# Splitting the second unit's heads into high and low parts for their scores, in an attention and MLP kernel

## The chip, the cores and the metric

The kernel runs on one core of a Trainium2 chip. The metric is the device time of one execution in microseconds (us). One core has TensorE (matmuls; PE in the profile, its weight loads PEld), VectorE (DVE), ScalarE (ACT), GpSimd (POOL) and SyncE (SP, which issues most of the transfers here). Each engine works through its own list of instructions in order and waits where an instruction needs another engine's or a transfer's result.

## What is computed

Attention with four sink columns and a sliding window of 128, then an MLP with a leaky step, all in float32. The inputs q, k and v have 4 batches, 8 heads, 768 positions and 64 numbers per position; the weights are float64 in memory.

```python
def _attn_ref(q, k, v, n_sink, window):
    scale = 1.0 / np.sqrt(D)
    scores = scale * np.matmul(q, k.transpose(0, 1, 3, 2))
    pos = np.arange(S)
    is_sink = pos[None, :] < int(n_sink)
    rel = pos[:, None] - pos[None, :]
    in_window = (rel >= 0) & (rel < int(window))
    scores = np.where(is_sink | in_window, scores, -1000000000.0)
    scores = scores - np.max(scores, axis=-1, keepdims=True)
    a = np.exp(scores)
    a = a / (np.sum(a, axis=-1, keepdims=True) + 1e-09)
    return np.matmul(a, v).astype(np.float32)
...
x = np.ascontiguousarray(attn_out.transpose(0, 2, 1, 3)).reshape(B * S, H * D)
h = x @ w_in                      # 3072 x 512 by 512 x 2048
g = np.maximum(0.01 * h, h)
return (g @ w_out).astype(np.float32)
```

## The kernel before, in words

**Units.** The work is cut into eight units: a unit is half a batch, 384 positions, that is three tiles of 128 queries, with all eight heads. Unit 0 is the first half of batch 0, unit 1, the "second unit" of this text, its second half. A first-half head needs 392 columns of keys and sinks, a second-half head 524 (`NK`); with 384 columns of queries, one head's tile `qk` has 776 or 908 columns. Queries and keys stand in it twice, in partitions 0 to 63 and 64 to 127.

**Two kinds of attention.** Units 0 and 1 (`EARLY = 2`, lines 419 to 439) work on float32: one float32 matmul per query tile, which the chip runs as two; as every product is summed twice over the 128 partitions, the scale is halved (`scale`, line 254). Their softmax covers 260 columns, two key blocks and the four sinks (`softmax_early`, lines 268 to 278), and their values are float32. From unit 2 on (`attend_late`) a head is split first (`split_head`, lines 224 to 234): ACT casts it to float32r (line 229), POOL subtracts the cast from the original for the lower copy of the keys (line 230) and for the queries (line 232). A score is then two float32r matmuls, of high and of low queries, against keys whose upper copy is high and whose lower copy is low (line 264), and the softmax there is narrower.

**Buffers of a head.** Loads are issued by SyncE (`load_head`, line 202). The tag `qkraw` has one buffer. The tag `qksp` has two, and holds split heads. In units 0 and 1, two of three heads are loaded straight into a `qksp` buffer, where the matmuls read them, and are called `qkn`; the third goes to `qkraw`. `load_next` (lines 217 to 222) sets how far ahead loads are issued: two heads ahead in units 0 and 1, one head ahead later.

**The MLP of a unit** goes in 16 steps (`fc`). In each, twelve matmuls into `h` (line 519), the leaky step `g` on ACT and VectorE (lines 526 and 527), a cast to its high part `gh` on ACT (528), and the low part `gl` by subtraction (529), which POOL does in unit 0's MLP and VectorE later; one step later nine matmuls into `o` (540).

**The weights** are decoded once, beside unit 0's MLP: SyncE loads 512 KB (lines 153 and 154), VectorE builds float32 from the float64 words in three instructions (170, 172, 174), ACT casts to the high part (178), POOL subtracts for the low part (179).

**Order.** Attention of unit 0 and the start of unit 1 run first; then unit u's MLP steps alternate with unit u + 1's attention, by counts of steps. TensorE's list is in the order in which the code issues it. The lists of ACT, VectorE, POOL and SyncE are set by the compiler's scheduler, from a time line of its own. In unit 1 probabilities are transposed on TensorE (lines 336 and 337) into one bank, which ACT's copy `pt` (338) must empty before the next pair. Names: `s` scores, `pe` the probabilities of an early head, `sk` its sink columns, `xh` and `xl` a unit's attention output in two parts, `wi` and `wo` the weights.

Of the kernel before, what the change touches and what calls it, by code (L numbers as in the profile page):

```python
# [21 lines left out]
B, H, S, D = 4, 8, 768, 64  # L22
# [5 lines left out]
T = 3  # L28
NU = 2 * B
EARLY = 2  # L30
TU = T * P
NSK = 4
SKR = P
# [4 lines left out]
NK = (3 * P + 2 * NSK, 4 * P + 3 * NSK)  # L38
NVB = (3, 4)
SCALE = 1.0 / D ** 0.5  # L40
# [71 lines left out]
def fast_path(ctx, tc, cpool, qk, vu, vs, w_in, w_out, out, ident, lim, masks, tri, diag, negm, wmin, wmax):  # L112
# [11 lines left out]

    wz = wpool.tile([P, TU], mybir.dt.bfloat16, name="wz")
    nc.vector.memset(wz, 0.0)
    zeros = iopool.tile([SKR, TU], F32, tag="io", name="zeros")
    nc.vector.memset(zeros, 0.0)
# [66 lines left out]
    def load_head(u, h):  # L195
        b, half = divmod(u, 2)
        early = u < EARLY
        if early and (u * H + h) % 3 < 2:
            raw = apool.tile([P, TU + NK[half]], F32, tag="qksp", name=f"qkn{u}_{h}")
        else:  # L200
            raw = apool.tile([P, TU + NK[half]], F32, tag="qkraw", name=f"qkraw{u}_{h}", bufs=1)
        nc.sync.dma_start(out=raw, in_=qk[half][b, h])
        raws[u, h] = raw
        if h % 2 == 0:
            if early and h % 4:
                vr = apool.tile([P, 4 * P], F32, tag="vsp", name=f"vn{u}_{h}", bufs=1)
            else:
                vr = iopool.tile([P, 4 * P], F32, tag="vraw", name=f"vraw{u}_{h}", bufs=1)
            eng = nc.scalar if early and u + h else nc.sync
            eng.dma_start(out=vr[:, 0:NVB[half] * P], in_=vu[half][b, h // 2])  # L210
            sr = apool.tile([SKR, P], F32, tag="vsraw", name=f"vsraw{u}_{h}", bufs=2)
            eng.dma_start(out=sr, in_=vs[b, h // 2])
            vraws[u, h] = (vr, sr)
# [2 lines left out]

    def load_next(u, h):
        n = u * H + h
        last = n + 2 if n + 2 < EARLY * H else n + 1
        while loaded[0] <= min(last, NU * H - 1):  # L220
            load_head(*divmod(loaded[0], H))
            loaded[0] += 1

    def split_head(u, h):
        half = u % 2
        n = NK[half]
        raw = raws.pop((u, h))
        sp = apool.tile([P, 2 * TU + NK[1]], F32R, tag="qksp", name=f"qksp{u}_{h}")
        nc.scalar.copy(out=sp[:, 0:TU + n], in_=raw[:, 0:TU + n])  # L229
        nc.gpsimd.tensor_tensor(out=sp[D:P, TU:TU + n], in0=raw[D:P, TU:TU + n],  # L230
                                in1=sp[D:P, TU:TU + n].bitcast(F32), op=ALU.subtract)
        nc.gpsimd.tensor_tensor(out=sp[:, TU + n:2 * TU + n], in0=raw[:, 0:TU],  # L232
                                in1=sp[:, 0:TU].bitcast(F32), op=ALU.subtract)
        return sp
# [13 lines left out]
    raws = {}  # L248
# [2 lines left out]
    warm = ps_h.tile([P, 512], F32, tag="h", name="warm")  # L251

    def scale(u):
        return -SCALE / 2 if u < EARLY else -SCALE

    def scores(u, h, j, parts, sp):
        k0, kn = KSL[u % 2][j]
        i = (h * T + j) % (SO + 1)
        if u == 0 and i:
            ps = ps_o.tile([P, 512], F32, tag=f"o{i - 1}", name=f"s{u}_{h}_{j}")  # L260
        else:
            ps = ps_s.tile([P, 512], F32, tag="s", name=f"s{u}_{h}_{j}")
        for c, off in enumerate(parts):
            nc.tensor.matmul(ps[:, 0:kn], lhsT=sp[:, off + j * P:off + (j + 1) * P],  # L264
                             rhs=sp[:, TU + k0:TU + k0 + kn], start=c == 0, stop=c == len(parts) - 1)
        return ps

    def softmax_early(u, h, j, ps, w, sm):
        half = u % 2
        if half or j:  # L270
            src, mask = ps[:, 0:W3], wide[0 if u == 0 and j == 1 else 1]
        else:
            src, w, mask = ps[:, 0:P], w[:, WM:], masks[0]
        col = (u * H + h) * T + j
        neg = negm[:, col:col + 1]
        anchor[0] = nc.vector.tensor_tensor_reduce(out=w, in0=src, in1=mask, scale=scale(u), scalar=3.0e38,  # L276
                                                   op0=ALU.add, op1=ALU.min, accum_out=neg)
        nc.scalar.activation(out=w, in_=w, func=AF.Exp, scale=-1.0, bias=neg, accum_out=sm[:, j:j + 1])

    def normalise_early(u, w, sm):  # L280
        nc.vector.tensor_scalar(out=sm, in0=sm, scalar1=1e-9, scalar2=None, op0=ALU.add)
        nc.vector.reciprocal(out=sm, in_=sm)
        for j in range(T):
            p = w[:, j, :] if u % 2 or j else w[:, j, WM:]
            if u:
                nc.scalar.mul(p, p, sm[:, j:j + 1])
            else:
                nc.vector.tensor_scalar(out=p, in0=p, scalar1=sm[:, j:j + 1], scalar2=None, op0=ALU.mult)

    def softmax(u, h, j, ps, w):  # L290
        if KSL[u % 2][j][1] == W3:
            nc.vector.copy_predicated(out=ps[:, WM:W3], mask=tri, data=ps[:, 0:P])
            src = ps[:, P:W3]
        else:
            src = ps[:, 0:P]
            w = w[:, NSK:]
        col = (u * H + h) * T + j
        sm = apool.tile([P, 1], F32, tag="sm", name=f"sm{u}_{h}_{j}", bufs=4)
        neg = negm[:, col:col + 1]
        anchor[0] = nc.vector.tensor_tensor_reduce(out=w, in0=src, in1=masks[min(T * (u % 2) + j, 2)],  # L300
                                                   scale=scale(u), scalar=3.0e38, op0=ALU.add, op1=ALU.min,
                                                   accum_out=neg)
        nc.scalar.activation(out=w, in_=w, func=AF.Exp, scale=-1.0, bias=neg, accum_out=sm)  # L303
        nc.vector.tensor_scalar(out=sm, in0=sm, scalar1=1e-9, scalar2=None, op0=ALU.add)
        nc.vector.reciprocal(out=sm, in_=sm)
        if NACT >> u & 1:
            nc.scalar.mul(w, w, sm)
        else:
            nc.vector.tensor_scalar(out=w, in0=w, scalar1=sm, scalar2=None, op0=ALU.mult)  # L309
# [21 lines left out]
    def tail_early(u, h, j, w, pt, sk):  # L331
        half = u % 2
        tp = slot()
        at = (P if half else 0) + (2 * j - 1) * P
        if half or j:
            nc.tensor.transpose(out=tp[:, 0:P], in_=w[:, j, 0:P], identity=ident)  # L336
            nc.tensor.transpose(out=tp[:, P:2 * P], in_=w[:, j, WM:], identity=ident)  # L337
            nc.scalar.copy(out=pt[:, 0, at:at + 2 * P], in_=tp[:, 0:2 * P])
        else:
            nc.tensor.transpose(out=tp[:, 0:P], in_=w[:, j, WM:], identity=ident)  # L340
            nc.scalar.copy(out=pt[:, 0, 0:P], in_=tp[:, 0:P])
        if j == T - 1:
            nj = T - 1 + half
            nc.gpsimd.tensor_copy(out=sk[:, 0:nj, h % 2], in_=w[:, T - nj:, P:WM])
# [20 lines left out]
    def sinks(u, pair, sk):  # L365
# [10 lines left out]
        sv = sv.rearrange("p j q -> p (j q)")  # L376
        if u < EARLY:
            return sv
# [6 lines left out]
    def values(u, h, pt, st, state):  # L385
# [5 lines left out]
        vv, sv = state["v"]  # L391
        if u < EARLY:
            if not odd:
# [11 lines left out]
        for c, (l, r, o, m) in enumerate(mms):  # L405
            nc.tensor.matmul(out[:, o:o + m], lhsT=l, rhs=r, start=c == 0, stop=c == len(mms) - 1,  # L406
                             skip_group_check=True)
        if u < EARLY:
            x = state["acc"][:, 0:TU]
# [8 lines left out]

    def attend_early(u, h, pend, state):
        odd = h % 2  # L420
        sp = raws.pop((u, h))
        state = state[h // 2 % 2]
        if not odd:
            state["v"] = vraws.pop((u, h))
            state["sk"] = apool.tile([P, T, 2, NSK], F32, tag="sk", name=f"sk{u}_{h // 2}")
        load_next(u, h)
        w = apool.tile([P, T, W3], F32, tag="pk", name=f"pe{u}_{h}", bufs=PKB)
        sm = apool.tile([P, T], F32, tag="sm", name=f"sm{u}_{h}", bufs=4)
        pt = apool.tile([P, 1, 2 * TU], F32, tag="pt", name=f"pt{u}_{h}")
        sk = state["sk"]  # L430
        state["pt", odd] = pt
        for j in range(T):
            softmax_early(u, h, j, scores(u, h, j, (0,), sp), w[:, j, :], sm)
            if j < T - 1:
                yield j
        normalise_early(u, w, sm)
        yield T - 1
        for j in range(T):
            pend.append((0, lambda j=j: tail_early(u, h, j, w, pt, sk)))
# [340 lines left out]
```

## Time and profile before

| | |
|---|---|
| median of 3 runs | 749.14 us (748.79 to 749.92) |
| the profiled execution's own time | 746.63 us |
| its span in the profile | 745.1 us |
| mean granted TensorE clock | 0.992 |
| loads of heads into `qkraw` | 26 of 388 KB (first halves), 27 of 454 KB (second halves) |
| split heads | 48 of 64 |

A row of the profile's groups gives the line of the kernel, the engine, the operation, the tile written and the tiles read with their shapes, how often it ran, then its busy time in us and the mean in ns, then the idle time of the engine just before these instructions and what ended it. The chain of waits goes back from the last instruction: at each step to what released it. A row of a time line has start and duration in us, engine, line, operation and count, and in brackets the idle time before it and what ended that. Matmuls overlap, so the duration of a single one is longer than the time for which it holds up the next; the chain gives the latter.

### The profile page before, as it was taken

What the parts mean: (1) busy time and instruction counts of PE and PEld (TensorE: products, weight loads), DVE (VectorE), ACT (ScalarE), POOL (GpSimd) and SP (SyncE); (2) the same over time, 40 slices, a digit from 0 to 9 for tenths busy, and PEclk for the clock granted to TensorE, in tenths of its full rate; (3) what the DMA queues carried; (4) which work ended last, traced back from release to release, by engine and by line L of the source; (5) the groups of instructions that cost most, each with busy time, mean ns of one, the idle gap of its engine ahead of it and who ended that gap; (6) DMA issues with size and microseconds to landing.
All of it is one profiled execution on the core that took longest, in us unless ns stands there. A gap on an engine that the chain in (4) does not pass through costs nothing.

```text
span 745.1 us, 12489 instructions
## 1 busy us (share of the span) xinstructions
PE 714.3 (96%) x3881; PEld 620.6 (83%) x3881; DVE 549.3 (74%) x1749; ACT 420.6 (56%) x1178; POOL 370.0 (50%) x500
## 2 busy tenths in 40 slices
PE   4788999899999999999999999999999999999996
PEld 3446777679999988999988888999889899989995
DVE  6856798847667888888888888889888978733222
ACT  3556567656665666666666666666666655522221
POOL 2303446745445677665666587665666555300000
PEclk9899999999999999999999999999999999999999
DMA  8744675413212343225333443334332321001001
GB/s 295 228 132 127 195 219 172 146 36 99 58 51 65 119 125 114 92 94 156 115 106 102 132 130 100 104 98 153 109 109 78 112 68 40 0 1 43 1 1 48
DMA packets 43755, 77.77 MB, mean 104 GB/s; under 512 B 3616, under 2 KB 26400, under 8 KB 43680
## 3 DMA queue, kind: packets, MB, share of 16 engines
q1 hardware_dynamic: 41520, 74.66, 32.1%
q10 hardware_dynamic: 2160, 2.23, 1.2%
q8 instruction: 33, 0.54, 0.3%
q14 instruction: 42, 0.34, 0.2%
HBM read 70.58 MB, written 6.29 MB: 103 GB/s over the span
## 4 chain that ended last, share of the span: by engine, by line
PE 84%; DVE 9%; ACT 3%; issue 1%; DMA 1%; ACTq 0%; SPq 0%; DVEq 0%
PE o L540 32%; PE h L519 31%; PE v L406 10%; PE s L264 7%; PE t L349 2%; DVE gl L529 2%; DVE zeroi L192 1%; PE t L336 1%; DMA qkn<-in_qk 1%; DVE g L527 1%; DVE pe L276 0%; DVE xf L415 0%; DVE pk L309 0%; PE t L370 0%; PE t L337 0%
## 5 line engine op out<-in xcount | busy, mean ns | idle before, releaser
L519 PE MATMUL h<-xh,wi 128*128 128x384 f32 x1024 | 314.9, 354 | 1.6 <-DVE g L527 1.6
L540 PE MATMUL o<-wo,gh 128*128 128x512 f32 x768 | 244.4, 399 | 0.0
L519 PEld LDWEIGHTS h<-xh,wi 128*128 128x128 f32 x1024 | 190.0, 188 | 16.6 <-issue 2.9
L519 PE MATMUL h<-xl,wi 128*128 128x384 f32 x512 | 172.5, 337 | 0.0
L540 PE MATMUL o<-wo,gl 128*128 128x512 f32 x384 | 151.5, 394 | 0.0
L540 PEld LDWEIGHTS o<-wo,gh 128*128 128x128 f32 x768 | 133.7, 188 | 18.2 <-issue 2.4
L318 POOL TENSOR_SCALAR_AFFINE_SELECT pt<-stg 128x256 fp32r<-128x256 f32 x240 | 101.3, 447 | 83.4 <-DVE stg L357 70.1
L527 DVE TENSOR_TENSOR g<-h,g 128x384 f32<-128x384 f32 x128 | 71.0, 555 | 62.2 <-ACT g L526 60.4
L529 DVE TENSOR_TENSOR gl<-g,gh 128x384 fp32r<-128x384 f32 x112 | 93.3, 833 | 16.5 <-ACT gh L528 15.0
L526 ACT ACTIVATE g<-h 128x384 f32<-128x384 f32 x128 | 62.2, 486 | 71.5 <-PE h L519 71.1
L519 PEld LDWEIGHTS h<-xl,wi 128*128 128x128 f32 x512 | 96.9, 189 | 3.6 <-DVE xl L475 0.2
L230 POOL TENSOR_TENSOR qksp<-qkraw,qksp 64x392 fp32r<-64x392 f32 (+1 forms) x48 | 58.4, 1218 | 64.2 <-issue 47.5
L540 PEld LDWEIGHTS o<-wo,gl 128*128 128x128 f32 x384 | 72.2, 188 | 16.7 <-DVE gl L529 0.3
L303 ACT ACTIVATE pk<-pk,negm 128x128 f32<-128x128 f32 (+1 forms) x144 | 58.1, 403 | 48.6 <-DVE negm L300 47.8
L528 ACT CAST gh<-g 128x384 fp32r<-128x384 f32 x128 | 65.7, 513 | 33.7 <-DVE g L527 31.3
L264 PEld LDWEIGHTS s<-qksp 128*128 128x128 f32 x288 | 53.3, 188 | 5.9
L264 PE MATMUL s<-qksp 128*128 128x260 f32 (+1 forms) x288 | 56.2, 277 | 0.0
L232 POOL TENSOR_TENSOR qksp<-qkraw,qksp 128x384 fp32r<-128x384 f32 x48 | 53.5, 1115 | 3.6
L356 ACT CAST stg<-t 128x128 fp32r<-128x128 f32 x120 | 30.8, 256 | 42.6 <-PE t L349 32.2
L406 PEld LDWEIGHTS v<-pt,vsp 128*128 128x128 f32 x336 | 45.1, 189 | 5.8 <-issue 3.3
L229 ACT CAST qksp<-qkraw 128x776 fp32r<-128x776 f32 (+1 forms) x48 | 42.8, 892 | 11.3 <-PE s L264 11.0
L309 DVE TENSOR_SCALAR pk<-pk,sm 128x132 f32<-128x132 f32 (+1 forms) x120 | 46.0, 383 | 2.4
(131 smaller groups left out, 1088.0 us busy)
## 6 DMA issues: line engine op xcount, KB each, us to landing
qkraw<-in_qk SPq DMA_DIRECT2D x27, 454.0 KB, 3.3
qkraw<-in_qk SPq DMA_DIRECT2D x26, 388.0 KB, 3.1
wiraw<-in_w_in SPq DMA_DIRECT2D x16, 512.0 KB, 3.9
woraw<-in_w_out SPq DMA_DIRECT2D x16, 512.0 KB, 4.0
ciraw<-in_w_in SPq DMA_DIRECT2D x16, 512.0 KB, 3.8
coraw<-in_w_out SPq DMA_DIRECT2D x16, 512.0 KB, 3.6
out<-ob SPq DMA_DIRECT2D x23, 256.0 KB, 2.0
vraw<-in_vu SPq DMA_DIRECT2D x12, 256.0 KB, 2.7
```

The source lines that it names most:

```text
L230: nc.gpsimd.tensor_tensor(out=sp[D:P, TU:TU + n], in0=raw[D:P, TU:TU + n], in1=sp[D:P, TU:TU + n].bitcast(F32), op=ALU.subtract)
L232: nc.gpsimd.tensor_tensor(out=sp[:, TU + n:2 * TU + n], in0=raw[:, 0:TU], in1=sp[:, 0:TU].bitcast(F32), op=ALU.subtract)
L264: nc.tensor.matmul(ps[:, 0:kn], lhsT=sp[:, off + j * P:off + (j + 1) * P], rhs=sp[:, TU + k0:TU + k0 + kn], start=c == 0, stop=c == len(pa ...
L303: nc.scalar.activation(out=w, in_=w, func=AF.Exp, scale=-1.0, bias=neg, accum_out=sm)
L318: nc.gpsimd.affine_select(out=out, in_=src, pattern=([[0, x]] if x > 1 else []) + [[sign, P]], base=-1 if prev else 0, channel_multiplier= ...
L406: nc.tensor.matmul(out[:, o:o + m], lhsT=l, rhs=r, start=c == 0, stop=c == len(mms) - 1, skip_group_check=True)
L519: nc.tensor.matmul(ph[:, 0:TU], lhsT=w[:, cs], rhs=x, start=cc == 0 and c == 0, stop=cc == NCC - 1 and c == 2)
L526: nc.scalar.mul(g, ph[:, 0:TU], 0.01)
L527: anchor[0] = nc.vector.tensor_tensor(out=g, in0=ph[:, 0:TU], in1=g, op=ALU.max)
L528: nc.scalar.copy(out=gh, in_=g)
L529: (nc.gpsimd if u == 0 else nc.vector).tensor_tensor(out=gl, in0=g, in1=gh.bitcast(F32), op=ALU.subtract)
L540: nc.tensor.matmul(po[t], lhsT=gg[:, tsl], rhs=w, start=f == 0 and c == 0, stop=f == NFC - 1 and c == 2)
```

## The change

A new constant `NATS = 1` says how many units read their heads in float32. Unit 0 stays as it was. Unit 1 is now treated in two ways: its softmax over 260 columns, its normalisation, its transposes and its float32 values stay; its heads are loaded into `qkraw`, split by `split_head`, and scored by two float32r matmuls per tile, with the whole scale.

```diff
+NATS = 1
...
     def load_head(u, h):
...
-        if early and (u * H + h) % 3 < 2:
+        if u < NATS and h % 3 < 2:
             raw = apool.tile([P, TU + NK[half]], F32, tag="qksp", name=f"qkn{u}_{h}")
         else:
             raw = apool.tile([P, TU + NK[half]], F32, tag="qkraw", name=f"qkraw{u}_{h}", bufs=1)
...
     def load_next(u, h):
         n = u * H + h
-        last = n + 2 if n + 2 < EARLY * H else n + 1
+        last = n + 2 if n + 2 <= NATS * H else n + 1
...
     def scale(u):
-        return -SCALE / 2 if u < EARLY else -SCALE
+        return -SCALE / 2 if u < NATS else -SCALE
...
     def attend_early(u, h, pend, state):
-        sp = raws.pop((u, h))
+        sp = raws.pop((u, h)) if u < NATS else split_head(u, h)
+        parts = (0,) if u < NATS else (0, TU + NK[u % 2])
...
-            softmax_early(u, h, j, scores(u, h, j, (0,), sp), w[:, j, :], sm)
+            softmax_early(u, h, j, scores(u, h, j, parts, sp), w[:, j, :], sm)
```

`split_head` is called for unit 1 as it stands for the later units:

```python
        sp = apool.tile([P, 2 * TU + NK[1]], F32R, tag="qksp", name=f"qksp{u}_{h}")
        nc.scalar.copy(out=sp[:, 0:TU + n], in_=raw[:, 0:TU + n])
        nc.gpsimd.tensor_tensor(out=sp[D:P, TU:TU + n], in0=raw[D:P, TU:TU + n],
                                in1=sp[D:P, TU:TU + n].bitcast(F32), op=ALU.subtract)
        nc.gpsimd.tensor_tensor(out=sp[:, TU + n:2 * TU + n], in0=raw[:, 0:TU],
                                in1=sp[:, 0:TU].bitcast(F32), op=ALU.subtract)
```

TensorE's list keeps its order; the 24 float32 scores of unit 1 become 24 pairs. In the lists of the other engines the new instructions are put in, and neighbours change places. Line numbers of the kernel after are one or two higher. Three places follow. The first is ACT's list where unit 0's MLP begins, before; `g_0`, `gh_0` are the first step's, `pe_1` is unit 1's head 1, `pt_0` a copy for head 0.

```order
L526 ACTIVATE g_0_663<-h_0_646 128x384
L278 ACTIVATE pe_1_622,sm_1_623<-pe_1_622,negm 128x260
L528 CAST gh_0_664<-g_0_663 128x384
L286 ACTIVATE pe_1_622<-pe_1_622,sm_1_623 128x260 x3
L178 CAST wi_686<-wif_682 128x512
L338 COPY pt_0_586<-t_706 128x256
```

The same place after:

```order
L528 ACTIVATE g_0_674<-h_0_657 128x384
L230 CAST qksp_3_878<-qkraw_3_754 128x908
L279 ACTIVATE pe_1_631,sm_1_632<-pe_1_631,negm 128x260
L530 CAST gh_0_675<-g_0_674 128x384
L179 CAST wi_698<-wif_694 128x512
L287 ACTIVATE pe_1_631<-pe_1_631,sm_1_632 128x260 x3
L339 COPY pt_0_584<-t_718 128x256
```

The cast of unit 1's head 3 stands between the first `g` and what followed it, and the weight cast has gone ahead of the normalisation. The second place is POOL's list from the last heads of unit 0 to the MLP's first low part `gl_0`, before:

```order
L344 COPY sk_2_397<-pe_5_442 128x2x4
L344 COPY sk_3_487<-pe_6_494 128x2x4
L344 COPY sk_3_487<-pe_7_532 128x2x4
L344 COPY sk_0_577<-pe_0_584 128x3x4
L529 TENSOR_TENSOR gl_0_665<-g_0_663,gh_0_664 128x384
```

And after:

```order
L345 COPY sk_2_397<-pe_5_442 128x2x4
L231 TENSOR_TENSOR qksp_0_575<-qkraw_0_488,qksp_0_575 64x524
L233 TENSOR_TENSOR qksp_0_575<-qkraw_0_488,qksp_0_575 128x384
L345 COPY sk_3_487<-pe_6_494 128x2x4
L345 COPY sk_3_487<-pe_7_530 128x2x4
L231 TENSOR_TENSOR qksp_1_621<-qkraw_1_580,qksp_1_621 64x524
L233 TENSOR_TENSOR qksp_1_621<-qkraw_1_580,qksp_1_621 128x384
L345 COPY sk_0_579<-pe_0_582 128x3x4
L231 TENSOR_TENSOR qksp_2_749<-qkraw_2_625,qksp_2_749 64x524
L233 TENSOR_TENSOR qksp_2_749<-qkraw_2_625,qksp_2_749 128x384
L231 TENSOR_TENSOR qksp_3_878<-qkraw_3_754,qksp_3_878 64x524
```

The subtracts of four heads stand ahead of `gl_0` (the fourth head's second one follows the last row). The third place is SyncE's list of loads, unit 1's heads 0 to 4 and the next weights, before:

```order
L202 DMA qkraw_0_488<-in_qk 128x908
L202 DMA qkn_1_530<-in_qk 128x908
L202 DMA qkn_2_578<-in_qk 128x908
L202 DMA qkraw_3_620<-in_qk 128x908
L202 DMA qkn_4_738<-in_qk 128x908
L153 DMA wiraw_829<-in_w_in 128x4x256
L154 DMA woraw_839<-in_w_out 128x1024
```

And after:

```order
L203 DMA qkraw_0_488<-in_qk 128x908
L203 DMA qkraw_1_580<-in_qk 128x908
L203 DMA qkraw_2_625<-in_qk 128x908
L203 DMA qkraw_3_754<-in_qk 128x908
L154 DMA wiraw_844<-in_w_in 128x4x256
L203 DMA qkraw_4_882<-in_qk 128x908
L155 DMA woraw_854<-in_w_out 128x1024
```

All loads of unit 1 share the one `qkraw` buffer, and head 4's load has moved behind one weight transfer.

## The prediction

> **What bounds the kernel now.** I read the head of the page first, then its chain of waits, then a table of busy times in stretches of 20 us around the second unit, last the instructions one by one. Of the page, the span, the busy times and the chain:
>
> ```profile
> span 745.1 us, 12489 instructions
> PE 714.3 (96%) x3881; PEld 620.6 (83%) x3881; DVE 549.3 (74%) x1749; ACT 420.6 (56%) x1178; POOL 370.0 (50%) x500
> ...
> PE 84%; DVE 9%; ACT 3%; issue 1%; DMA 1%; ACTq 0%; SPq 0%; DVEq 0%
> ```
>
> TensorE sets the end, so what counts is what the change does to TensorE's time or makes it wait for. The second unit's scores run from 50 to 138 us. In these stretches stand the busy times of PE, PEld, DVE, ACT and POOL (instructions in brackets), then the granted clock, the transfers' share and GB/s:
>
> ```profile
> 40.00:60.00 20.00, 17.23 (x83) 10.18 (x82) 10.11 (x45) 11.96 (x44) 0.76 (x4) 1.00 0.44 127
> 60.00:80.00 20.00, 18.07 (x95) 14.79 (x93) 16.88 (x37) 13.04 (x34) 9.71 (x10) 1.00 0.59 178
> 80.00:100.00 20.00, 19.54 (x98) 15.70 (x98) 14.82 (x34) 12.00 (x32) 9.98 (x10) 1.00 0.66 184
> 100.00:120.00 20.00, 20.00 (x101) 15.58 (x99) 15.86 (x36) 12.19 (x33) 10.45 (x11) 1.00 0.65 197
> 120.00:140.00 20.00, 19.30 (x96) 14.71 (x94) 15.93 (x33) 12.86 (x32) 13.11 (x13) 1.00 0.68 211
> ...
> 180.00:200.00 20.00, 20.00 (x114) 18.11 (x114) 13.22 (x47) 13.22 (x39) 10.22 (x15) 1.00 0.16 44
> ```
>
> From 80 us on TensorE is nearly full at full clock: a shorter score shows in the end time. From 40 to 80 us it has 4.7 us of gaps: there the order of the other engines decides.
>
> **What the change takes away.** A score of 260 columns is two matmuls before and after. The chain gives what the pair holds up TensorE, first in float32 (second unit), then split (third unit):
>
> ```profile
> 69.91 0.44 PE s L264 x2
> ...
> 162.26 0.24 PE s L264 x2
> ```
>
> That is 0.20 us for each of 8 heads x 3 tiles: 24 x 0.20 = 4.8 us less, the whole gain.
>
> **What it adds.** The third unit and those after it split their heads already, so the prices are there: cast, lower half of the keys, queries, then the load of one head (454 KB, issue to landing; the second row is from 36 to 160 us alone).
>
> ```profile
> L229 ACT CAST qksp<-qkraw 128x908 fp32r<-128x908 f32 x24 | 22.7, 948 | 4.7 <-PE s L264 4.7
> L230 POOL TENSOR_TENSOR qksp<-qkraw,qksp 64x524 fp32r<-64x524 f32 x24 | 32.9, 1371 | 33.3 <-issue 25.3 <-POOL pt L318 7.9
> L232 POOL TENSOR_TENSOR qksp<-qkraw,qksp 128x384 fp32r<-128x384 f32 x48 | 53.5, 1115 | 3.6
> qkraw<-in_qk SPq DMA_DIRECT2D x27, 454.0 KB, 3.3
> qkraw<-in_qk SPq DMA_DIRECT2D x3, 454.0 KB, 3.7
> ```
>
> By volume this fits: ACT gets 8 x 0.95 = 7.6 us, POOL 8 x (1.37 + 1.12) = 19.9 us, over some 80 us in which (60 to 140) POOL has 43 busy and ACT 50. What does not fit by itself is the sequence. All loads of the unit now go into one buffer, which is free only after the second subtract of the head before. A head thus costs at least 3.3 + 0.95 + 1.37 + 1.12 = 6.7 us (7.1 at 3.7 us a load) in a row. Where TensorE takes longer than that per head it is hidden. At the unit's start it does not, and there ACT's order has a cast ahead of work that TensorE needs. The rows for this, SyncE's loads, ACT, TensorE and POOL of before:
>
> ```profile
> 40.00 0.33 SPq L202 DMA_DIRECT2D qkraw<-in_qk  x1
> 43.47 5.86 SPq L202 DMA_DIRECT2D qkn<-in_qk  x2
> ...
> 43.30 0.51 ACT L278 ACTIVATE pe<-pe,negm 128x260 f32<-128x260 f32 x1
> 43.72 0.19 ACT L278 ACTIVATION_READ_ACCUMULATOR pe<-pe,negm 128x1 f32 x1
> ...
> 51.38 0.51 ACT L278 ACTIVATE pe<-pe,negm 128x260 f32<-128x260 f32 x1 [0.52 <-DVE negm L276]
> 51.80 0.19 ACT L278 ACTIVATION_READ_ACCUMULATOR pe<-pe,negm 128x1 f32 x1
> ...
> 61.49 0.49 ACT L526 ACTIVATE g<-h 128x384 f32<-128x384 f32 x1 [0.82 <-PE h L519]
> ...
> 63.47 0.51 ACT L528 CAST gh<-g 128x384 fp32r<-128x384 f32 x1 [0.46 <-DVE g L527]
> ```
>
> ```profile
> 50.16 0.60 PE L264 MATMUL s<-qkraw 128*128 128x260 f32 x2
> ...
> 53.87 0.70 PE L264 MATMUL s<-qkn 128*128 128x260 f32 x2 [0.20 <-DVE negm L276]
> ...
> 58.74 0.44 PE L519 MATMUL h<-xh,wi 128*128 128x384 f32 x1
> ...
> 66.43 0.33 PE L336 MATMUL t<-ident,pe 128*128 128x128 f32 x1 [0.34 <-ACT pt L338]
> ...
> 67.17 0.39 PE L540 MATMUL o<-wo,gl 128*128 128x512 f32 x1
> ...
> 68.09 0.60 PE L264 MATMUL s<-qkn 128*128 128x260 f32 x2
> ...
> 67.04 0.33 SPq L154 DMA_DIRECT2D woraw<-in_w_out  x1
> ...
> 64.06 1.01 POOL L529 TENSOR_TENSOR gl<-g,gh 128x384 fp32r<-128x384 f32 x1 [6.81 <-ACT gh L528]
> ```
>
> Head by head, counted in the second unit:
>
> Head 0: its load stands where it stood (40.00, landed 43.3). The cast comes behind the exponential that ends at 43.9, is done at 44.9, the subtracts at 47.4. TensorE wants it at 50.16: hidden, with 2.8 us to spare; a load that lands later than that costs TensorE the rest in full.
>
> Head 1: its load went out with the pair of 43.47, now only at 47.4; it lands at 50.7. The cast stands behind the exponential that ends at 52.0: done at 52.9, the subtracts at 55.4. TensorE wants it at 53.87, and its second matmul waits for the last subtract: about 1.0 us late, 0.8 when the next, shorter score is through. The MLP thus begins near 59.5 where it began at 58.74.
>
> Head 2: load at 55.4, landed 58.7 to 59.1, cast until 59.7 or 60.1, subtracts until 62.2 or 62.6. Its first score stands at 68.09: hidden by over 5 us.
>
> Head 3: load at 62.2 to 62.6, landed 65.5 to 66.3. Its scores are far off, but ACT takes its cast right behind the first leaky step (61.49), ahead of an exponential, the cast gh, a weight cast, a normalisation and the copy that frees the transposes' bank. ACT stands still from about 63 until the load is there, casts for 0.95, does the exponential in 0.70, and comes to gh at 67.2 to 67.9 where it was there at 63.47: 3.7 to 4.5 us late, I take 4.1. The copy and the transpose at 66.43 come as much later, and TensorE's list has nothing else ahead of them. The MLP's low part gl, now behind head 3's subtracts on POOL, is done near 66.9 + 2.5 + 1.0 = 70.4; TensorE wants it at 67.17 + 4.1 = 71.3: hidden, by 0.9. On SyncE the load of head 4 still stands ahead of the weight transfer of 67.04, but now waits for head 3's subtracts, 69.4: 2.4 us later for the weights while the stage is 4.1 late, so hidden too.
>
> So at this transpose TensorE is 4.1 us late, with the first six cheaper scores in that. The other 18 give back 18 x 0.20 = 3.6. That leaves +0.5.
>
> After it, heads 4 to 7 put four casts ahead of ACT's copies. Bounds: TensorE's waits for these copies fall away by half of what they are below, -1.0; or all four casts reach TensorE, 4 x 0.95 = +3.8. From 180 to 200 us casts of this kind run under a TensorE that is busy 20.00 of 20, so I stay near nothing: +0.5. The transfers add no bytes. The last wait of the stage, for the weights' decode, stays:
>
> ```profile
> PE t L336 <- DVE wof L174: 2.0, 1, 2.0
> PE t L336 <- ACT pt L338: 1.9, 4, 0.7
> ```
>
> Sum: +0.5 + 0.5 = +1.0 us. The profiled execution took 746.63 us (its span of 745.1 and 1.5 around it), which makes 747.6; the median of the runs, 749.14, lies 2.5 above it, so the forecast is 750.1 us. A change of 0.2%, 1.5 us, is about what a measurement of this kernel can tell from none.
>
> A rule speaks against this change. Of the two subtracts' kind POOL needs 1115 ns for 128x384, VectorE 577:
>
> ```profile
> L475 DVE TENSOR_TENSOR xl<-xf,xh 128x384 fp32r<-128x384 f32 x20 | 11.5, 577 | 0.0
> ```
>
> The Trainium skill ("GPSIMD Engine Reference", section 4.1 Engine selection) gives elementwise work to VectorE, since GpSimd is about two times slower with two inputs; the trace agrees, 1115 against 577. By it, subtracts on VectorE would shorten the two links before head 3's cast by some 1.2 us each, and the sum would be about -1.4 (an estimate).
>
> **The rivals.**
>
> Faster: ACT's halt costs TensorE nothing, because loads land sooner than 3.3 us or the waits of 60 to 80 us (1.9) take it up. Then only head 1's 0.8 is lost (five scores in it) and 19 x 0.20 = 3.8 won: -3.0, 746.1 us. For it: TensorE waits there already. Against it: the cast is ahead of gh in a list that keeps its order.
>
> Slower: POOL becomes late in every head. The gl of 64.06 is done at 65.07 and wanted at 67.17: 2.1 us of room, and a head's subtracts take 2.49. If heads 4 to 7 each lose these 0.4 and their cast's 0.95, that is 5.4 us, and with +0.5 before it 755.0 us. It decides when gl ends after the last matmul ahead of its own. Against it: POOL has half its time free.
>
> VectorE held up by POOL. One small step of VectorE, three numbers per row, takes 0.16 us, but 0.78 and 0.86 where a POOL subtract runs beside it:
>
> ```profile
> 63.35 0.16 DVE L281 TENSOR_SCALAR sm<-sm 128x3 f32<-128x3 f32 x1
> 75.73 0.78 DVE L281 TENSOR_SCALAR sm<-sm 128x3 f32<-128x3 f32 x1
> 140.29 0.86 DVE L281 TENSOR_SCALAR sm<-sm 128x3 f32<-128x3 f32 x1 [0.25 <-ACT pe L278]
> ...
> 75.19 1.29 POOL L179 TENSOR_TENSOR wo<-wof,wo 128x512 fp32r<-128x512 f32 x1
> ```
>
> With 19.9 us more of POOL all eight could take 0.7 more, 5.6 us of VectorE; a third of it in the decode that TensorE waits for would add 2 us: 752.1 us. The Trainium skill ("SBUF — State Buffer", section SBUF: two separate sides) calls the port pair that the two share an exclusive lock, held for a whole instruction; the trace agrees, the step of 75.73 ends at 76.51, with POOL's subtract at 76.48.
>
> **How the numbers follow.** Forecast 0.56; its own range -1 to +3, so 0.35 of it within 1.5 us and 0.21 above. Faster rival 0.25. POOL late 0.12, slower. VectorE held up 0.07, 0.05 slower and 0.02 within. Together faster 0.25, same 0.37, slower 0.38. The range takes in the faster rival's -3.0 with a little of its spread and most of the way to the slower one's +5.9: 745.6 to 754.0.
>
> **What would show it.** In the profile of after: scores of the second unit at 0.24 in the chain; ACT waiting some 2 to 3 us for a DMA ahead of the cast near 63 to 66 us; TensorE waiting some 3 us for ACT's copy near 67 to 70 us, and 1 us for POOL near 54; after 80 us no more gaps than before. The forecast is wrong if ACT's cast finds its load landed, if TensorE has waits for gl or weights between 80 and 140 us, or if the wait of 2.0 near 148 us grows.

## The result, and the profile after

The changed kernel takes 753.19 us, median of 4 runs (751.2 to 754.42), the kernel before 748.97 beside it: a ratio of 1.0053, 95% interval 1.0037 to 1.0069. It is slower by about half a per cent. The forecast was 750.1, within a range of 745.6 to 754.0; so the time lies inside the range, but near its upper edge, and what the profile shows is not what the forecast had described.

The head of the page and the shares of the chain, after:

```profile
span 749.3 us, 12515 instructions
PE 717.0 (96%) x3881; PEld 621.7 (83%) x3881; DVE 551.4 (74%) x1749; ACT 425.9 (57%) x1186; POOL 388.4 (52%) x516
...
PE 84%; DVE 8%; ACT 4%; issue 1%; POOL 1%; DMA 1%; ACTq 0%; SPq 0%; POOLq 0%; DVEq 0%
```

ACT has 5.3 us more than before and POOL 18.4, near the 7.6 and 19.9 that were forecast. But TensorE, which lost 4.8 us of scores, is busy 2.7 us longer. Where that is from shows in the stretches of 20 us, with the columns as in the prediction (PE, PEld, DVE, ACT, POOL, then the granted clock):

```profile
40.00:60.00 20.00, 16.69 (x70) 9.47 (x69) 11.25 (x43) 13.77 (x44) 5.90 (x9) 0.85 0.32 99
60.00:80.00 20.00, 17.21 (x75) 13.85 (x75) 10.82 (x24) 9.97 (x26) 9.27 (x10) 0.81 0.34 119
80.00:100.00 20.00, 19.32 (x100) 14.83 (x100) 15.93 (x36) 12.89 (x32) 13.45 (x13) 1.00 0.65 196
100.00:120.00 20.00, 19.95 (x105) 15.53 (x104) 16.69 (x36) 13.36 (x34) 14.50 (x15) 1.00 0.71 221
120.00:140.00 20.00, 18.83 (x100) 14.89 (x99) 17.66 (x38) 14.12 (x37) 16.50 (x16) 1.00 0.71 224
```

The granted clock is 0.85 and 0.81 in the first two rows; before it was 1.00 in both. In finer stretches (TensorE's busy time, then the clock), after:

```profile
52.00:54.00 2.00, 1.51 (x8) 1.00 0.00 0
54.00:56.00 2.00, 1.18 (x3) 0.53 0.00 0
56.00:66.00 10.00, 10.00 (x27) 0.50 0.38 126
66.00:68.00 2.00, 2.00 (x9) 0.55 0.00 0
```

From 54.1 to 67.8 us TensorE runs at half clock: 27 matmul records fill ten microseconds that held 42 before. The fall comes just ahead of head 1's first score, 0.4 us into TensorE's wait for its subtract. TensorE's rows there, after:

```profile
51.35 0.51 PE L265 MATMUL s<-qksp 128*128 128x260 f32 x2 [0.64 <-DVE negm L277]
...
54.33 0.58 PE L265 MATMUL s<-qksp 128*128 128x260 f32 x1 [0.58 <-POOL qksp L231]
55.40 0.58 PE L265 MATMUL s<-qksp 128*128 128x260 f32 x1 [0.49 <-POOL qksp L233]
55.92 2.40 PE L407 MATMUL v<-pt,vn 128*64 128x256 f32 x6
...
63.38 0.69 PE L521 MATMUL h<-xh,wi 128*128 128x384 f32 x1
```

The wait for POOL's two subtracts is there, 0.58 + 0.49 us, as forecast (1.0). Behind it the same six matmuls of the values take 2.40 us that took 1.30 before:

```profile
54.51 1.30 PE L406 MATMUL v<-pt,vn 128*64 128x256 f32 x6
```

and the MLP's first matmul stands at 63.38 where it stood at 58.74: 4.6 us late, where 0.8 was forecast. ACT's list in the place where it was to stand still, after:

```profile
68.00 0.49 ACT L528 ACTIVATE g<-h 128x384 f32<-128x384 f32 x1 [1.50 <-PE h L521]
68.39 0.94 ACT L230 CAST qksp<-qkraw 128x908 fp32r<-128x908 f32 x1
```

The cast of head 3 comes right behind the first leaky step, as forecast, but at 68.39, and it waits for nothing: the load, issued at 61.9, has landed in the time that the slow TensorE took. TensorE's waits from 40 to 165 us, after:

```profile
PE t L337 <- ACT pt L339: 3.3, 4, 1.2
PE t L337 <- DVE wof L175: 1.8, 1, 1.8
```

For ACT's copies it waits 1.4 us more than before, and 1.2 at the longest, not 3 or more. The wait for the weights' decode is nearly the same (1.8, before 2.0). The scores are as short as forecast, and casts and subtracts of the later heads stand on the chain between 80 and 105 us. From the chain of waits of 68 to 140 us:

```profile
79.99 0.26 PE s L265 x2
80.27 0.47 ACT qksp L230
81.35 1.33 POOL qksp L231
82.77 1.01 POOL qksp L233
...
89.15 0.24 PE s L265 x2
95.24 0.85 ACT qksp L230
...
104.75 0.54 ACT qksp L230
```

To compare kernels stage by stage, I take the start of the MLP's 1st, 25th and 145th `h` matmul from TensorE's rows. Between the last two lie the last 17 of the 24 scores, all but the first of heads 2 to 7. By the forecast's terms they save 17 x 0.20 = 3.4 us and the later heads lose 0.5 of it.

| us | 1st | 25th | 145th | 25th to 145th | span |
|---|---|---|---|---|---|
| before | 58.7 | 69.2 | 138.9 | 69.7 | 745.1 |
| after | 63.4 | 76.2 | 143.8 | 67.7 | 749.3 |

The loss is complete by the 25th matmul (7.0 us); 2.0 us come back, not 2.9; from the 145th on the two nearly keep their distance, 4.9 there and 4.2 at the end. Head 0's second score still stands at the same time in both, 51.40 before and 51.35 after; where other runs come to it earlier or later, I count from there.

### The profile page after: what moved, and what is told of

Its sections match the earlier page's. It is cut to its first block, busy times and chain, and to the rows that moved or that the text cites. A ratio compares the mean times of both kernels' runs of the same rounds, so it can differ in the third digit from the quotient of the medians.

```text
span 749.3 us, 12515 instructions
## 1 busy us (share of the span) xinstructions
PE 717.0 (96%) x3881; PEld 621.7 (83%) x3881; DVE 551.4 (74%) x1749; ACT 425.9 (57%) x1186; POOL 388.4 (52%) x516
## 4 chain that ended last, share of the span: by engine, by line
PE 84%; DVE 8%; ACT 4%; issue 1%; POOL 1%; DMA 1%; ACTq 0%; SPq 0%; POOLq 0%; DVEq 0%
PE h L521 32%; PE o L542 32%; PE v L407 11%; PE s L265 6%; PE t L350 2%; DVE gl L531 2%; DVE zeroi L193 1%; PE t L337 1%; ACT qksp L230 1%; DMA qkn<-in_qk 1%; ACT pe L279 1%; DVE g L529 1%; DVE xf L416 0%; DVE pk L310 0%; PE t L371 0%
## 5 line engine op out<-in xcount | busy, mean ns | idle before, releaser
L231 POOL TENSOR_TENSOR qksp<-qkraw,qksp 64x524 fp32r<-64x524 f32 (+1 forms) x56 | 69.0, 1232 | 78.6 <-issue 49.3
L265 PEld LDWEIGHTS s<-qksp 128*128 128x128 f32 x336 | 62.3, 190 | 10.1 <-DVE negm L277 1.2
L265 PE MATMUL s<-qksp 128*128 128x260 f32 (+1 forms) x336 | 67.3, 281 | 1.8 <-DVE negm L277 0.6
L233 POOL TENSOR_TENSOR qksp<-qkraw,qksp 128x384 fp32r<-128x384 f32 x56 | 61.6, 1100 | 4.2
L230 ACT CAST qksp<-qkraw 128x908 fp32r<-128x908 f32 (+1 forms) x56 | 50.4, 900 | 14.8 <-PE s L265 13.8
```

## The experiments

**The theories.** The clock: a pause near 54 us, of about a microsecond, lets TensorE's granted clock fall to half for some 12 us, which costs about 5 us; without it, ACT's stop for head 3's load would appear, as forecast, and cost about as much. The rival: the casts and subtracts cost it, as work that ACT and POOL do in the same stretch. Twelve kernels ran in three groups of four, each group with the kernel before beside it (medians 749.42, 748.3 and 749.25); each ratio is to the kernel before of the same group.

The first theory is tested with spare matmuls: bf16, 128x384, on zeros, into a PSUM bank whose contents nobody reads. They add TensorE work and take nothing away.

```
def fill(n):
    if n:
        pw = ps_o.tile([P, 512], F32, tag="o0", name=f"fill{len(fills)}")
        ...
        for _ in range(n):
            nc.tensor.matmul(pw[:, 0:TU], lhsT=wz[:, 0:P], rhs=wz, start=True, stop=True)
```

**Fourteen spare matmuls** in the changed kernel, ahead of scores of heads 0 and 1:

```
+FILL = (0, 4, 4), (6, 0, 0)
...
+            if u == 1 and h < 2:
+                fill(FILL[h][j])
             softmax_early(u, h, j, scores(u, h, j, parts, sp), w[:, j, :], sm)
```

> The changed kernel with 14 spare matmuls (bf16, 128x384, of zeros, into a bank of o that is free there) in TensorE's list: 4 each ahead of the second and third score of the second unit's head 0, 6 ahead of head 1's first score. They remove no wait and no work; the scheduler also moves a few rows of ACT, POOL and SyncE there. Theory (clock): in the changed kernel TensorE's granted clock falls to 0.50 from about 54 to 67 us because TensorE pauses around 51 to 55 us; with the pauses filled it stays at 1.00, the MLP begins near 60 to 61 us instead of 63.4, and the time is 747 to 749 us against 753.2 of the changed kernel. Rival (ACT and POOL): the loss is the splits' work on ACT and POOL, and the clock is a bystander: the time stays at 753 us or rises by up to 1 us with the spare matmuls.

749.66 us, 1.0004 of before (0.9991 to 1.0017): the whole loss is gone, by adding work. The clock is 1.00 from 54 to 76 us. But this kernel differs in a second way: the scheduler moved rows of ACT's list, the cast of head 3 to a later place among them, and head 3's subtracts on POOL behind the MLP's first low part. So the next one holds the lists.

**Two spare matmuls**, `FILL = (0, 1, 0), (1, 0, 0)`, with the lists of ACT, POOL, VectorE and SyncE exactly those of after:

> The same with two spare matmuls alone, one ahead of the second score of head 0, one ahead of head 1's first; the lists of all other engines are those of the changed kernel. 0.32 us of spare work fills little of the 2 us of pauses. Theory (clock): near the limit, so either the drop stays (753 us) or it is gone (748 us), together with the clock in the table of windows: time and clock go together. Rival (ACT and POOL): 753 us whatever the clock does.

754.91 us, 1.0079 (1.0063 to 1.0094): slower than after. The clock held, 1.00 from 54 to 70 us, and the MLP began at 61.2. Then came what the forecast had described. ACT's cast of head 3 and TensorE's longest wait in this kernel:

```profile
68.08 0.95 ACT L231 CAST qksp<-qkraw 128x908 fp32r<-128x908 f32 x1 [3.65 <-DMA qkraw<-in_qk]
```

```profile
PE t L338 <- ACT pt L340: 7.1, 4, 4.9
```

ACT stands still for 3.65 us for the load, and TensorE 4.9 at the transpose behind its copy (forecast: 2 to 3, and 4.1). After this pause the clock fell all the same, later. TensorE's busy time and clock:

```profile
70.00:72.00 2.00, 0.00 (x0) 1.00 0.01 4
72.00:74.00 2.00, 0.75 (x3) 0.59 0.85 242
74.00:76.00 2.00, 2.00 (x6) 0.50 1.03 357
```

So the two losses stand in each other's way: in after, the low clock delays TensorE until the load has landed; hold the clock up, and the stop is there.

**The same fourteen in the kernel before**, the control:

> Control: the kernel before with the same 14 spare matmuls at the same places. Its clock is 1.00 from 40 to 76 us already, so there is nothing to keep up. Theory (clock): no gain, 749 to 751 us (14 x 0.16 = 2.2 us of matmuls, 1 us of it inside waits). Rival (ACT and POOL): the same. If it is clearly faster than 749, spare matmuls do something else than hold the clock there, and the first run does not count for the theory.

750.37 us, 1.0028 (1.0009 to 1.0047). In the profile (749.36 us) the clock stays up, and the spare matmuls win nothing. Four of the twelve runs, with a mean clock of 0.986 and 0.987, take 753.15 to 754.89; where these lose is not shown.

**Heads 0 and 1 in float32**, as before the change, heads 2 to 7 split:

```
-NATS = 1
+NATH = 10
...
-        if u < NATS and h % 3 < 2:
+        if u * H + h < NATH and (u * H + h) % 3 < 2:
...
```

> The changed kernel with heads 0 and 1 of the second unit left in float32, loaded ahead as in the kernel before; heads 2 to 7 are split. This takes away TensorE's wait for POOL near 54 us and makes TensorE busier there. Theory (clock): the clock stays at 1.00; 18 of the 24 shorter scores are left, 18 x 0.20 = 3.6 us, less up to 1.5 us for casts and subtracts of six heads in TensorE's way: 745.5 to 747.5 us. Rival (ACT and POOL): six of eight splits cost six eighths of the loss: 749.0 + 3.2 = 752 us.

749.26 us, 0.9999 (0.9982 to 1.0017). TensorE waits no more for POOL at 54 us, the clock is 1.00 from 40 to 76, and 25th to 145th takes 67.5 us, near after's 67.7. With six of eight heads split, the loss is gone: it came with the first two, though their casts, subtracts, shorter scores and order of loads went together here. No more is won, and neither expectation held: the theory had 745.5 to 747.5, the rival 752.

**Only heads 0 and 1 split**, the rest as before, was to be the other half of that test:

> The kernel before with only heads 0 and 1 of the second unit split (cast, two subtracts, shorter scores); heads 2 to 7 stay float32 and load ahead as before, so nothing of ACT's stop for head 3's load can occur. Theory (the clock): TensorE waits about 1 us for POOL at 54 us, the granted clock falls to 0.50 from about 54 to 67 us, the 24 v and s matmuls there take twice as long, the MLP starts near 63.4 instead of 58.7 us, and no more than 6 x 0.20 = 1.2 us comes back: 753 to 755 us, 4 to 5 us above the kernel before, although only a quarter of the change is in it. Rival (the work on ACT and POOL costs by its volume, a quarter of it here): 749.5 to 751 us, the clock at 1.00 from 54 to 67.

758.09 us, 1.0113 (1.0089 to 1.0138), slower than either theory said. The edit brought a wait of its own. SyncE's list now has head 2's load ahead of head 1's, and that one waits for its buffer until 50.59; both go out together, and ACT's cast of head 1 waits for the load until 56.04. TensorE's longest wait there is 3.8 us:

```profile
PE s L268 <- DVE sm L285: 3.8, 1, 3.8
```

The row names VectorE, but VectorE's step L285 had itself waited for ACT. The clock then is 0.50 to 0.55 from 58 to 72 us. With **two spare matmuls** in this kernel

> The kernel of e5_two_split with two spare bf16 matmuls of 128x384 on TensorE ahead of heads 0's second and 1's first score; the lists of all other engines are the same. Theory (the clock): the spare matmuls keep the granted clock at 1.00 from 54 to 70 us as in e1b_two_fills, the wait for POOL of about 1 us stays, no stop of ACT follows since head 3's load is early: 749 to 750.5 us, 4 us under e5_two_split. Rival (work on ACT and POOL): spare matmuls add 0.3 us and win nothing: as e5_two_split or above it.

it takes 757.49 us (1.0111, 1.0089 to 1.0133): two matmuls of 0.16 us do nothing against a pause of 4.5. As a test of a short pause both kernels failed. What they show is that a quarter of the change can cost 9.8 us, over twice what all of it costs, so its price does not go by the volume of casts and subtracts alone; the order of the loads, which this edit changed, can cost more.

**The clock held and head 3's cast put later.** The kernel with two spare matmuls, and the cast behind the copy that frees the transposes' bank, five places down ACT's list (a wait on the same engine only):

```
-        nc.scalar.copy(out=sp[:, 0:TU + n], in_=raw[:, 0:TU + n])
+        behind = copied.get((1, 0, 1)) if (u, h) == (1, 3) else None
+        with tc.issue_after(behind.ins) if behind else nullcontext():
+            nc.scalar.copy(out=sp[:, 0:TU + n], in_=raw[:, 0:TU + n])
```

> The kernel of e1b_two_fills (all eight heads split, two spare matmuls that keep the clock up at 54 us) with head 3's cast put five places later in ACT's list, behind the copy that frees the transposes' bank; SyncE's load of head 4 moves behind one weight load. Theory (ACT's stop at head 3's load is what e1b_two_fills lost, and the clock fell after it): the wait of 4.9 us for ACT's copy goes to under 1.5 us, the granted clock stays at 1.00 from 54 to 80 us, the MLP's 25th matmul starts near 71.5 instead of 78.0 us: 748 to 750 us, 5 to 6 us under e1b_two_fills. Rival (the sum of casts and subtracts costs it, wherever they stand): 753 to 755 us.

747.93 us, 0.9995 of before (0.9978 to 1.0011), where the kernel with the two spare matmuls alone had 1.0079: some 6 us less, with every cast and subtract still in it. The scheduler moved more than the cast: head 3's subtracts on POOL go behind the MLP's first low part, and SyncE's load of head 4 behind one more weight transfer; what each of these is worth is not separated. The cast of head 3 finds its load landed, and the longest wait for ACT's copies is 1.2 again:

```profile
67.00 0.95 ACT L234 CAST qksp<-qkraw 128x908 fp32r<-128x908 f32 x1
```

```profile
PE t L342 <- ACT pt L344: 2.5, 4, 1.2
```

The rival had 753 to 755 here; it is out as the cause of the loss.

**The late cast without spare matmuls** completes the square. All lists but TensorE's are those of the kernel above:

> The changed kernel with head 3's cast five places later in ACT's list, as in e6_late_cast, but without the two spare matmuls: the lists of ACT, POOL, VectorE and SyncE are those of e6_late_cast. Theory (two separate losses, the clock at 54 us and ACT's stop; the one hides the other): the clock falls at 54 us as in the changed kernel, head 3's load is landed by then anyhow, the later cast wins nothing: 751.5 to 754 us in most runs, and 747 to 749 in runs whose clock is 0.985 or more. Rival (the cast's place is all): 747.5 to 749 us, as e6_late_cast, whatever the clock.

750.68 us, 1.0028 (1.0009 to 1.0046), and this median hides groups. Of its 12 runs, four have a mean clock of 0.987 and take 747.84 to 748.33 us; four have 0.979 or 0.980 and take 752.96 to 754.01; the other four, at 0.982 and 0.983, take 750.06 to 752.06. One program, one order of work, and 5.5 us between the first two groups: a clock lower by 0.0075 over 748 us is 5.6 us (an estimate from these numbers). The profiled execution is one of the first group. TensorE waits for POOL as in after, even longer:

```profile
54.80 0.39 PE L269 MATMUL s<-qksp 128*128 128x260 f32 x1 [0.59 <-POOL qksp L234]
55.87 0.39 PE L269 MATMUL s<-qksp 128*128 128x260 f32 x1 [0.68 <-POOL qksp L236]
56.19 1.29 PE L411 MATMUL v<-pt,vn 128*64 128x256 f32 x6
...
60.21 0.44 PE L525 MATMUL h<-xh,wi 128*128 128x384 f32 x1
```

and yet its clock holds, and the six matmuls take 1.29:

```profile
54.00:56.00 2.00, 0.72 (x4) 1.00 0.00 0
56.00:66.00 10.00, 8.41 (x42) 1.00 0.44 127
```

So the pause does not force the clock down. By the mean clock it fell somewhere in eight of these twelve runs (the mean does not tell where), with the two spare matmuls in one of twelve (0.980, 752.2 us; the others 0.985 to 0.990, 745.82 to 749.59), with fourteen in none of twelve (0.985 to 0.991). The rival, that the cast's place is all, would have had every run near 748.

**The changed kernel again**, beside it on the same chip:

> The changed kernel as it is, once more, beside the next three on one chip. Theory (the clock decides): its runs have a mean granted clock of 0.980 to 0.983 and take 751 to 754.5 us, median 753; if a run happens to keep the clock at 54 us (0.985 and more), ACT's stop for head 3's load appears in its place and it is no faster than 753. Rival (work on ACT and POOL): the same median, but with no relation between a run's clock and its time.

753.13 us, 1.0052 (1.0038 to 1.0066), the first result over again. Four runs at 0.979 and 0.980 take 752.89 to 754.77; two at 0.985 and 0.987 take 751.58 and 752.33. Where its clock stays up it gains little, as the stop at head 3's load would have it; no profile of such a run of this kernel was taken, only of the one with two spare matmuls. The profile taken here (754.77 us) shows where the fall comes; a row with TensorE's clock, and two of its rows:

```profile
54.00:56.00 2.00, 1.54 (x7) 0.96 0.19 62
...
57.06 0.58 PE L265 MATMUL s<-qksp 128*128 128x260 f32 x1
58.13 0.59 PE L265 MATMUL s<-qksp 128*128 128x260 f32 x1 [0.49 <-POOL qksp L233]
```

A mean of 0.96 over 2 us puts the fall at 55.8 us: 1.2 us before head 1's first score, and before TensorE had waited for POOL at all. So the wait for POOL is not what makes the clock fall; the theory's "pause near 54 us" can only be the waits ahead of it, 0.64 and 0.27 us here.

**The subtracts on VectorE**, the rule that the prediction weighed:

```
+        eng = nc.vector if u < EARLY else nc.gpsimd
...
-        nc.gpsimd.tensor_tensor(out=sp[D:P, TU:TU + n], in0=raw[D:P, TU:TU + n],
+        eng.tensor_tensor(out=sp[D:P, TU:TU + n], in0=raw[D:P, TU:TU + n],
...
```

> The changed kernel with the second unit's 16 subtracts on VectorE instead of POOL (the rule on the engine for elementwise work); ACT's and VectorE's lists are reordered by the scheduler in some places. The rule, with the clock theory: a head's two subtracts take about 1.3 instead of 2.3 us, head 1's upper half is ready some 1 us sooner, TensorE's wait at 54 us is under 0.3 us and the clock stays at 1.00 until head 3's load, which is then about 1 to 2 us late or hidden: 747.5 to 750 us. Rival (VectorE, 74% busy, is itself waited for at 50 to 60 us: its steps come 1.3 us later per head): a pause of TensorE for VectorE in the place of POOL's, the clock falls all the same: 752 to 755 us.

755.34 us, 1.0079 (1.0053 to 1.0104). Head 1's subtracts took 0.70 and 0.56 us in place of POOL's 1.29 and 0.99, and no score waits for POOL. But TensorE pauses for VectorE and ACT in the same place, and the clock falls at 55.6 us. TensorE's rows:

```profile
53.02 0.33 PE L338 MATMUL t<-ident,pe 128*128 128x128 f32 x1 [0.69 <-ACT pt L343]
...
54.34 0.51 PE L266 MATMUL s<-qksp 128*128 128x260 f32 x2 [0.64 <-DVE negm L278]
```

Two such waits, 0.69 for ACT and 0.64 for VectorE, stand in the kernel before too, at 49.88 and 51.40 us, under a clock of 1.00; they alone do not bring it down. Ten of the 12 runs have a clock of 0.976 to 0.979 and take 753.47 to 757.27; the two at 0.988 and 0.989 take 748.22 and 747.86. The rule of the Trainium skill ("GPSIMD Engine Reference", section 4.1 Engine selection) holds for the price of the step, and the kernel is no faster by it; by the two groups of runs, what the time hangs on is the clock. The prediction's estimate by that rule was -1.4 us against before; measured is a loss.

**Spare matmuls wherever TensorE is idle early.** Before and after both have low clock from 16 to 23 and 32 to 37 us, behind pauses of 3.1 us for VectorE. If such stretches cost time everywhere, there are some 5 us to win (10.2 us at half clock in before). To the kernel that matched before, 18, 18 and 10 spare matmuls were added, ahead of two transposes of the first unit and of the one near 147 us:

```
+SPARE = {(0, 1, 0): 18, (0, 3, 0): 18, (1, 7, 2): 10}
...
         tp = slot()
+        for _ in range(SPARE.get((u, h, j), 0)):
+            nc.tensor.matmul(tp[:, 0:TU], lhsT=wz[:, 0:P], rhs=wz, start=True, stop=True)
```

> The kernel of e6_late_cast with 46 more spare bf16 matmuls where TensorE stands idle in both kernels: 18 each ahead of the transposes that wait for VectorE near 14 and 29 us, 10 ahead of the one near 147 us; the scheduler moves some weight casts and weight loads of the first unit with it. Theory (pauses drop the clock, here too): the clock stays at 1.00 from 14 to 38 us and at 148 us, which gives back up to 6 us at half clock, 3 us each less what the moved casts cost: 742 to 746 us, faster than both kernels. Rival (these drops have another cause, the transfers of 300 to 400 GB/s at that time): clock of 0.50 near 18 and 34 us as before, 747 to 749 us.

749.88 us, 1.0022 (1.0006 to 1.0038). And the kernel before with the same:

> The kernel before with the same 46 spare matmuls near 14, 29 and 147 us: the control. Theory (pauses drop the clock): 743 to 747 us, so that e9_all_fills is within 2 us of it. Rival (another cause of the early drops): 748 to 750 us.

751.12 us, 1.0016 (0.9995 to 1.0037). The first half of the theory held: these drops come from the pauses, not from the transfers. From the kernel before with spare matmuls, TensorE's busy time, clock, transfers' share and GB/s:

```profile
14.00:16.00 2.00, 2.00 (x14) 1.00 1.08 403
16.00:18.00 2.00, 1.50 (x9) 1.00 0.79 278
...
34.00:36.00 2.00, 2.00 (x9) 1.00 0.82 263
40.00:46.00 6.00, 4.48 (x14) 0.56 0.56 202
```

and the same stretches of the kernel before as it is:

```profile
14.00:16.00 2.00, 0.00 (x0) 0.94 1.08 400
16.00:18.00 2.00, 0.45 (x1) 0.50 0.97 337
...
34.00:36.00 2.00, 2.00 (x6) 0.50 0.80 301
40.00:46.00 6.00, 4.96 (x27) 1.00 0.65 190
```

The second half fell: the median is no shorter. Two of TensorE's rows, with the spare matmuls:

```profile
38.25 0.83 PE L265 MATMUL s<-qkn 128*128 128x128 f32 x4
41.52 0.45 PE L343 MATMUL t<-ident,pe 128*128 128x128 f32 x1 [2.45 <-DVE pe L289]
```

and before:

```profile
41.15 0.83 PE L264 MATMUL s<-qkn 128*128 128x128 f32 x4
42.32 0.30 PE L340 MATMUL t<-ident,pe 128*128 128x128 f32 x1 [0.35 <-DVE pe L288]
```

TensorE comes to its scores 2.9 us earlier and then waits 2.45 us for VectorE, where it waited 0.35: VectorE sets the end of this stage, and most of the early half clock was hidden behind it: the transpose starts 0.8 us earlier, not 2.9. And the new pause drops the clock at 41, in a place where it had been full. This profile is one of three runs with a mean clock of 0.988, which take 752.75 to 754.08 us; four at 0.996 and 0.997 take 746.85 to 748.50, up to 2.4 under the median of before, so by the mean clock a little may be won where the new drop does not come. No profile of such a run was taken. Nor is an early drop always hidden: in the profile of the changed kernel again the first one lasted 10.2 us, in after 6.8, and the scores around it took 2.0 us longer (19.81 to 31.19 us, in after 19.06 to 28.41). The scheduler also moved weight casts and loads of the first unit, and what these cost is not separated.

## Why the prediction was right and wrong

The range held the time; the forecast itself, 750.1, was 3.1 us low. The path to it left out one term and mis-sized another, and one of its own signs of being wrong came: ACT's cast of head 3 found its load landed.

**The gain, 24 x 0.20 us: right.** The pairs take 0.24 in the chain. What comes back between the 25th and the 145th matmul was mis-sized: 2.0 us of 3.4, so 1.4 are lost there, not 0.5. TensorE's gaps from 80 to 140 us, where none more were forecast, grew from 1.2 to 1.9 us; that is 0.7 of it, and the rest is not located. On the chain of that stretch stand 1.86 us of casts and 2.34 of subtracts, where the forecast had bounds of -1.0 to +3.8 and named the casts alone; how much of the 1.4 is theirs was not tested.

**Head 0 and head 2, hidden: right.** No wait for them shows.

**Head 1, "about 1.0 us late, 0.8 when the next, shorter score is through": right as a wait, and the step that failed in what it left out.** The wait is 1.07 us and in its place. From head 0's second score to the MLP's first matmul it is 7.3 us before, and 8.4 in three kernels with all eight heads split whose profiles show a clock of 1.00 there (two spare matmuls; the late cast with them; the late cast alone): 1.1 us more, 0.9 at the 13th matmul. In after it is 12.0. The step let the MLP begin "near 59.5" and so priced the matmuls behind the wait at the granted clock of 1.00 that the profile of before shows. A fall of the clock had no term. It cost 5.5 us: from head 0's second score to the 13th matmul 18.4 us in after, 12.9 in each of the three.

**Head 3, ACT stopped by the load, 4.1 us: right as a mechanism, absent in this profile.** The forecast reckoned the load's landing against a TensorE at full speed. With the clock held up it came, 3.65 us on ACT and 4.9 on TensorE. In after, the low clock hid it. The sum came out near by chance: one loss of 4.1 was counted that did not occur, and one of 5.5 occurred that was not counted.

**The sum, as measured at the 145th matmul:** +0.9 for head 1 and +5.5 for the clock (6.3 us at the 13th matmul, as after was 0.05 ahead at head 0's second score), +0.6 from the 13th to the 25th, where ACT's copy is waited for (6.4 us, before 5.7), less 2.0: +4.9. The forecast had 4.1 at the transpose behind ACT's halt, which covers head 1's 0.8, and nothing for the clock; then less 3.6, plus 0.5.

**The rivals.** Faster, because ACT's halt costs nothing: the halt did not occur in after, and it was not faster. POOL late in every head: not seen, TensorE waits for its scores' subtracts in head 1 only. VectorE held up by POOL: the wait for the decode did not grow.

**The cause, shown:** the loss goes with the clock and, where the clock holds, with ACT's stop. With all casts and subtracts in place, undoing both losses gives 747.93 against 748.3; undoing one leaves 754.91 (the clock alone) or 750.68 in groups (the cast alone). No kernel's median beat before clearly: the best ratio, 0.9995, cannot be told from 1.

**Open:** what makes the clock fall. In every trace its changes lie whole multiples of 3.41 us apart (last section). In the 3.41 us before such a moment, TensorE was busy 2.02 us in after (to 54.14), 2.20 in the changed kernel again (to 55.83) and 1.89 with the subtracts on VectorE (to 55.55), where the clock fell; 2.40 in the late cast alone (to 54.18), 2.35 in it with spare matmuls (to 54.03) and 2.57 in the kernel before (to 53.32), where it held. But from 60.15 to 63.56 us in the kernel before 1.82 us were enough, so the busy time alone does not decide. Against head 0's second score the moment lay 2.4 us later in the late cast alone and 2.8 in after, with the same work on TensorE up to there. Such a shift could let one program fall in some runs and not in others; that is not tested.

## What to carry to other kernels

A wait on TensorE has two prices, its own length and what the granted clock does behind it: look at the clock in 2 us stretches wherever TensorE gets a new pause or less work, and count the matmuls behind it once at full and once at half speed. A loss can hide another; when an experiment that removes a cause makes the kernel slower, look for the wait that the cause had covered, and remove both before judging. And where the runs of one kernel spread over several microseconds, sort them by their mean clock before comparing medians. It does not always tell: in the first group the kernel before took 747.86 to 750.46 us at 0.986 and 0.987, and 747.33 to 751.08 at 0.989 and 0.990.

## What the runs showed of the hardware

The clock fell without a long pause. In after the longest single waits between 50 and 56 us are 0.64, 0.58 and 0.49 us, and TensorE is busy 1.2 to 1.5 us of each 2. It then stayed at 0.50 for 13.7 us, though TensorE was busy 10.00 of 10 from 56 to 66.

The clock changed only at certain moments. In each of the fourteen traces its changes lie whole multiples of 3.41 us apart; in after at 16.59, 23.42, 33.66, 37.07, 54.14 and 67.79 us. Stretches at half clock lasted 3.4, 6.8, 10.2 or 13.7 us. Where these moments lie against the kernel's work differs from run to run.

The Trainium skill ("TensorE: Matmul & The Clock Gate", Part 1) has the clock halved after an idle window of about 3.4 us and back after one busy window of that length, by a window that runs free of the kernel. The spacing of 3.41 us and its shift from run to run agree with such a window. The drops behind the early pauses of 3.1 us and behind the pause of 4.9 come near the first; the one at 54 us does not. Three stretches of 3.4 us with TensorE busy throughout, from 57.6 to 67.8 us, passed before the clock came back, which does not fit the second; from 19.2 to 22.6 us in the kernel before one was enough. The same page of the Trainium skill puts the cost of a ramp under 1% of a typical span. The runs agree: one drop costs 5.5 us of 748, 0.7%. But that is more than the 4.8 us that the change could win.
